# Attention and a two-layer MLP on one core: two blocks take w_in and x in float32, and w_in is split one block later

## The chip, the cores and the metric

The kernel runs on one core of one Trainium2 chip. A core has five engines with instruction queues of their own: TensorE (PE in the profile; its weight loads are PEld), VectorE (DVE), ScalarE (ACT), GpSimd (POOL) and SyncE (SP), which here only issues DMAs. The metric is the device time of one execution in microseconds (us); lower is better.

## The reference, cut to what matters

```python
q, k, v: (4, 8, 576, 64)          # batch, heads, sequence, head size; float32
q_rot, k_rot = rotate(q), rotate(k)
scores = np.matmul(q_rot, k_rot.transpose(0, 1, 3, 2)) / 8
attn = np.exp(scores - np.max(scores, axis=-1, keepdims=True))
attn = attn / (np.sum(attn, axis=-1, keepdims=True) + 1e-09)
attn_out = np.matmul(attn, v)
x = attn_out.transpose(0, 2, 1, 3).reshape(2304, 512)
h = x @ w_in                                             # w_in (512, 2048)
g = np.maximum(h, 0.0) + alpha * np.minimum(h, 0.0)
return g @ w_out                                         # w_out (2048, 512)
```

All in float32. The kernel is handed q and k with a turned copy beside them, and the bits of w_in and w_out as 64-bit floats.

## The kernel before, in words

**Tiles and blocks.** The 2304 tokens are 18 tiles of 128, and two tiles are a block: nine blocks. A block's attention is 16 heads: PE makes the scores (L655, or L683 where a tile holds the end of one batch and the start of the next), DVE their maximum (`mx`, L707), ACT the exponential (L716), ACT or DVE the float16 high part `pp` (L721, L354), DVE its low part (L735), a DMA transposes both (L739), and PE multiplies with v (L746). `normalise` divides (`y`, L761), splits y into two float16 parts `xs` (L765 or L766 high, L768 low), and a DMA transposes these to `xt` (L775).

**The two layers.** `expert(i, j)` does step j of 16 of block i. Layer 1 takes 128 columns of w_in: 12 float16 matmuls of 256 columns (L789: for each of four slices high by high, high by low, low by high) into the one buffer `h`; ACT and DVE make the leaky relu `r` (L800, L803), and not until both have read `h` can the next step's layer 1 begin. Layer 2 is in float32 for blocks 0 and 1 (L809, two matmuls of 512 columns, each of which the trace shows as two rows), and in three products of rounded parts from block 2 on (L827). `split(j)` makes w_out's parts in block 1's time (L609 high, L613 low; the low part is written into the buffer of step j-1, so it waits until block 1's layer 2 has used that).

**The weights.** `weights(g)`, for each quarter g: four pieces of w_in are loaded (L530), made into float32 by three integer operations on DVE (`to_f32`: L508, L513, L517), bounded (ACT takes absolute sums, L538; then a small chain on DVE and PE gives one scale `wsc` for the quarter), scaled and rounded to float16 on ACT (L582), and the low part is made on DVE (L586). The 64-bit buffer `wraw` (eight of them) is held until then. Four pieces of w_out are loaded, made into float32, and scaled by the bound on ACT (L599).

**What sets the order.** Every operation is handed to a planner (`Plan`) with a due time `at` (in steps; `slot(i, j)` is that of step j of block i, less an entry of the table `PRM`) and a cost for each engine that may do it. The planner plays the program through and writes one fixed order for each engine; engines with a choice get the operation that way. On the chip each engine runs its order as written and waits with semaphores.

Of the kernel before, what the change touches and what calls it, by code (L numbers as in the profile page):

```python
# [9 lines left out]
F32 = mybir.dt.float32  # L10
# [24 lines left out]
PRM = {"qd": 7.03, "qd0": 3.48, "vl0": 32.45, "wl": 12.02, "wl2": 12.07, "wb": 10.45, "wb2": 4.87, "ws": -0.7, "ws2": -0.08, "kl": 40.87, "vl": 40.84, "lead": 3.61, "flow": 4, "pen": -3.74, "ph": 1.2, "xlo": 1.8, "kd": 2.73, "pl": 1.01, "wlo": 16.77, "wg": 3.2, "bk": 1500, "lead1": 2.25, "ph0": 3.06, "nb": 1, "wh": 8.51, "lw": 3.8, "pvd": 4.03, "pw": 3.28, "la": 2, "lv": 1, "nks": 5, "nvv": 5, "ka": 2.03, "va": 0.1, "vc": -2.76, "vp": 1.47, "qa": 0.5, "qr": 78.54, "tqk": 1340, "l2d": 3.34, "tl2": 1400, "nos": 2, "nr": 2, "fo": 4, "fi": 4, "gh": 21.96, "gl": 10.88, "gh0": -1.64, "gl0": 1.86, "tp": 0, "nf": 2, "sh": 8.29, "sl": 2.28, "tl": 0, "wpe": 0, "vpe": 1, "wk": 4.09}  # L35
# [192 lines left out]
def t_dve(n, ap=0, fast=False):  # L228
    return 68 + (0.521 if fast else 1.042) * n + 60 * ap
# [6 lines left out]
def t_dma(size):  # L236
    return size / 360.0
# [3 lines left out]
def attention_moe(ctx: ExitStack, tc: tile.TileContext, q, k, v, w_in, w_out, alpha, tab, eye, out):  # L241
# [89 lines left out]
    e16_b = single("e16", [128, 128], F32)  # L331
# [5 lines left out]
    xu_T = tag("xu", 3, [128, 1], F32)  # L337

# [10 lines left out]
    def small(at, fn, reads=(), writes=()):  # L349
        op(at, {DVE: 75}, lambda e: fn(), reads=reads, writes=writes, port=False)  # L350
# [11 lines left out]
    def bound(at, cm, dst, acc, ps):  # L362
# [158 lines left out]

    def weights(g):
        at = slot(0, FG * g)
        wm, m, ps = wm_T.new(), column(at - 8), pair_T[1 + g % 2].new()
        raws = []
        for c in range(KC):
            raw, token = wr_T.new(), flow.new()
            raws.append((raw, token))
            op(at - PRM.get('wl', 16) + PRM.get('wg', 2) * g, {SP: t_dma(128 * 512 * 8)},
               lambda e, raw=raw, c=c: nc.sync.dma_start(  # L530
                   out=raw().rearrange("p f w -> p (f w)").bitcast(I64), in_=w_in[c, g]),
               writes=[raw, token])
        for c, (raw, token) in enumerate(raws):
            tmp = lambda c=c: wi_b().bitcast(I32)[:, c, g]
            dst = lambda raw=raw: raw()[:, :, 1]
            to_f32(at - PRM.get('wb', 5), raw, tmp, (wi_b, (c, g)), dst, raw, token)
            op(at - PRM.get('wb', 5), {ACT: t_act(512, ap=1)},
               lambda e, raw=raw, c=c, tmp=tmp: nc.scalar.activation(  # L538
                   out=tmp().bitcast(F32), in_=raw().bitcast(F32)[:, :, 1], func=ACTF.Abs,
                   accum_out=wm()[:, c:c + 1]),  # L540
               reads=[raw], writes=[(wi_b, (c, g)), (wm, c)])
        op(at - 4, {DVE: 80}, lambda e: nc.vector.tensor_reduce(out=m()[:, 0:1], in_=wm(), axis=AX.X, op=ALU.max),
           reads=[(wm, c) for c in range(KC)], writes=[m], port=False)
        bound(at - 4, m, lambda: we_b()[:, g:g + 1], (we_b, g), ps)
        we, wsc, wus = (lambda b=b: b()[:, g:g + 1] for b in (we_b, wsc_b, wus_b))
        scale_of(at - 4, wsc, (wsc_b, g), we, (we_b, g))
        small(at - 4, lambda: scalar(wus(), we(), 2.0**-14, None, ALU.mult), reads=[(we_b, g)], writes=[(wus_b, g)])
        by_pe = g < PRM["wpe"]
        if by_pe:
            dg = diagonal(at - 4, wsc, (wsc_b, g))  # L550
        for c, (raw, _) in enumerate(raws):
            f = lambda raw=raw: raw().bitcast(F32)[:, :, 1]
            t = lambda c=c: wi_b()[:, c, g]
# [428 lines left out]
```

## Time and profile before

| | |
|---|---|
| median of 3 runs (lowest to highest) | 688.65 us (685.98 to 691.06) |
| the profiled execution, its own time | 684.13 us |
| its span, first to last instruction | 682.3 us |
| mean granted TensorE clock | 0.955 of 2.4 GHz |
| busy in the span | PE 89%, DVE 74%, ACT 50%, POOL 27% |

The profile is one execution. A row of its timeline gives start, length, engine, line, operation and, in brackets, the time that the engine stood idle before it and what ended that. Lengths are from the start of one instruction to its end; one instruction may start a little before the end of the one ahead of it on its engine.

### The profile page before, as it was taken

The numbers are of one execution on the slowest core, as the hardware profiler recorded it, in microseconds if no ns is written. First come the engines' busy times: TensorE is split into PE (matmuls) and PEld (weight loads), VectorE is DVE, ScalarE is ACT, GpSimd is POOL, SyncE is SP. The second block draws the span as 40 slices with busy tenths as digits, with TensorE's granted clock in tenths as the row PEclk, the third lists the DMA queues.
The fourth block names the chain that finished last, engine by engine and source line by source line (L and its number), as shares of the span: only waits on it lengthen the run. The fifth ranks groups of instructions, "written<-read, shape, count | busy, mean of one in ns | idle before, by whom it ended". The sixth has DMA issues, their size and how long they took to land.

```text
span 682.3 us, 13828 instructions
## 1 busy us (share of the span) xinstructions
PE 608.4 (89%) x5384; PEld 443.8 (65%) x5384; DVE 507.9 (74%) x879; ACT 339.9 (50%) x766; POOL 181.0 (27%) x145
## 2 busy tenths in 40 slices
PE   0656678779899999999999999999999999999997
PEld 0334444455656567777767777677777777777775
DVE  5998999999778776768886586777866667765332
ACT  3536747539743435545654545464545445543322
POOL 4763000204642212126623222253211202110000
PEclk9966669979999999999999999999999999999999
DMA  8999898695985745468896456774445555462000
GB/s 302 312 233 226 159 292 214 193 272 121 222 167 108 135 86 132 86 114 184 198 211 106 99 118 103 112 183 100 84 69 105 110 78 86 101 119 54 32 0 32
DMA packets 209009, 96.47 MB, mean 141 GB/s; under 512 B 191792, under 2 KB 196016, under 8 KB 208944
## 3 DMA queue, kind: packets, MB, share of 16 engines
q1 hardware_dynamic: 208944, 95.59, 63.0%
q8 instruction: 42, 0.69, 0.4%
q14 instruction: 23, 0.19, 0.1%
HBM read 41.56 MB, written 4.72 MB: 68 GB/s over the span
## 4 chain that ended last, share of the span: by engine, by line
PE 68%; DMA 18%; DVE 10%; issue 1%; ACT 1%; SPq 1%; POOL 0%; ACTq 0%; DVEq 0%; POOLq 0%
PE h L789 24%; PE pair L827 21%; DMA pt<-pp 14%; PE v L746 8%; PE pair L655 8%; PE pair L809 5%; PE pair L683 2%; DVE kraw L390 1%; DMA qr<-in_q_dram 1%; DMA kraw<-in_k_dram 1%; DVE pp L735 1%; DVE mx L707 1%; DVE wi L586 1%; DMA wraw<-in_moe_w_out_dram 1%; DVE wraw L517 1%
## 5 line engine op out<-in xcount | busy, mean ns | idle before, releaser
L789 PE MATMUL h<-xt,wi 128*128 128x256 f16 x1728 | 231.4, 277 | 11.1 <-DVE r L803 10.6
L789 PEld LDWEIGHTS <-wi 128*128 128x128 f16 x1728 | 156.3, 99 | 72.3 <-issue 53.5
L716 ACT ACTIVATE e<-pair,mx 128x576 f32<-128x576 f32 x144 | 105.6, 736 | 87.7 <-DVE mx L707 83.5
L735 DVE SCALAR_TENSOR_TENSOR pp<-e,pp 128x576 f16<-128x576 f32 x144 | 126.1, 882 | 8.1 <-ACT pp L721 7.0
L803 DVE SCALAR_TENSOR_TENSOR r<-r,beta,h 128x256 f32<-128x256 f32 x144 | 68.7, 477 | 75.9 <-ACT r L800 75.6
L800 ACT ACTIVATE r<-h 128x256 f32<-128x256 f32 x144 | 55.1, 383 | 132.4 <-PE h L789 129.5
L746 PE MATMUL v<-vv,pt 128*128 128x64 f16 (+1 forms) x2240 | 92.6, 199 | 30.1 <-DMA pt<-pp 29.8
L746 PEld LDWEIGHTS <-pt 128*128 128x128 f16 (+1 forms) x2240 | 84.0, 104 | 51.3 <-DMA pt<-pp 41.6
L707 DVE TENSOR_REDUCE mx<-pair 128x1 f32<-128x576 f32 x144 | 103.2, 750 | 11.7 <-PE pair L655 10.3
L827 PE MATMUL pair<-wh,gh 128*128 128x512 f32 x224 | 96.0, 429 | 0.7 <-ACT gh L817 0.7
L655 PE MATMUL pair<-ks,qn 64*128 64x288 f32 x512 | 89.4, 453 | 7.2 <-ACT e L716 6.2
L827 PE MATMUL pair<-wh,gl 128*128 128x512 f32 x224 | 87.6, 391 | 0.8 <-POOL gl L820 0.8
L827 PE MATMUL pair<-wo,gh 128*128 128x512 f32 x224 | 88.2, 394 | 0.0
L820 POOL TENSOR_TENSOR gl<-r,gh 128x256 fp32r<-128x256 f32 x49 | 48.3, 986 | 116.5 <-ACT gh L817 80.1
L655 PEld LDWEIGHTS pair<-ks,qn 64*128 64x128 f32 x512 | 48.8, 196 | 35.5 <-issue 12.5
L721 ACT ACTIVATE pp<-e 128x576 f16<-128x576 f32 x90 | 61.1, 681 | 15.8 <-DMA pt<-pp 14.8
L817 ACT ACTIVATE gh<-r 128x256 fp32r<-128x256 f32 x97 | 40.4, 416 | 51.0 <-PE pair L827 33.9
L809 PE MATMUL pair<-wo,r 128*128 128x512 f32 x128 | 61.7, 607 | 0.0
L768 POOL TENSOR_TENSOR xs<-y,xs 128x512 f16<-128x512 f32 (+1 forms) x19 | 27.8, 1463 | 109.9 <-DVE xs L766 85.9
L827 PEld LDWEIGHTS pair<-wh,gl 128*128 128x128 f32 x224 | 42.0, 188 | 11.2 <-POOL gl L820 1.6
L827 PEld LDWEIGHTS pair<-wh,gh 128*128 128x128 f32 x224 | 42.2, 189 | 10.1 <-issue 1.9
L820 DVE TENSOR_TENSOR gl<-r,gh 128x256 fp32r<-128x256 f32 x63 | 28.7, 456 | 26.2 <-ACT gh L817 25.5
(77 smaller groups left out, 555.3 us busy)
## 6 DMA issues: line engine op xcount, KB each, us to landing
kraw<-in_k_dram SPq DMA_DIRECT2D x16, 576.0 KB, 4.6
qr<-in_q_dram SPq DMA_DIRECT2D x18, 512.0 KB, 4.2
wraw<-in_moe_w_in_dram SPq DMA_DIRECT2D x16, 512.0 KB, 5.5
wraw<-in_moe_w_out_dram SPq DMA_DIRECT2D x16, 512.0 KB, 5.6
vraw<-in_v_dram SPq DMA_DIRECT2D x16, 320.0 KB, 4.4
out_dram<-os SPq DMA_DIRECT2D x18, 256.0 KB, 2.2
pt<-pp SPq DMA_TRANSPOSE x144, 3.4
vv<-vv SPq DMA_DIRECT2D x32, 64.0 KB, 2.2
```

The lines of the kernel that those rows point to most:

```text
L655: nc.tensor.matmul(out=ps[h]()[:, x, :HS], lhsT=qn()[r, p], rhs=kt()[r, x * HS:(x + 1) * HS], start=True, stop=True)
L707: lambda e: nc.vector.tensor_reduce(out=mx()[a:z], in_=ps()[a:z, :, :HS], axis=AX.XY, op=ALU.max, negate=True),
L716: lambda e: nc.scalar.activation(out=ex()[a:z].rearrange("p (x c) -> p x c", x=2), in_=ps()[a:z, :, :HS], func=ACTF.Exp, bias=mx()[a:z], a ...
L721: lambda e: nc.scalar.activation(out=pp()[a:z, 0], in_=ex()[a:z], func=ACTF.Copy, scale=1.0 if early else E_SC) if e == ACT
L735: lambda e: nc.vector.scalar_tensor_tensor(out=pp()[a:z, 1], in0=ex()[a:z], scalar=E_SC, in1=pp()[a:z, 0], op0=ALU.mult, op1=ALU.subtract),
L746: nc.tensor.matmul(out=v_b()[c:d, 2 * p + g], lhsT=pt()[:, s, o:o + d - c], rhs=vt()[:, g, w], start=(n == 0), stop=(n == len(order) - 1))
L789: nc.tensor.matmul(out=ps(), lhsT=wi_b()[:, kk, j // FG, w, f], rhs=x()[:, y * KC + kk], start=(kk == 0 and n == 0), stop=(kk == KC - 1 an ...
L800: lambda e: nc.scalar.activation(out=g(), in_=ps(), func=ACTF.Relu, scale=-1.0),
L803: lambda e: nc.vector.scalar_tensor_tensor(out=g(), in0=g(), scalar=beta_b()[:, j:j + 1], in1=ps(), op0=ALU.mult, op1=ALU.add),
L809: nc.tensor.matmul(out=po()[:, x], lhsT=g()[:, x * 128:(x + 1) * 128], rhs=wf[j](), start=(j == 0), stop=(j == KF - 1))
L820: lambda e: ENG[e].tensor_tensor(out=gl(), in0=g(), in1=gh().bitcast(F32), op=ALU.subtract),
L827: nc.tensor.matmul(out=po()[:, x], lhsT=s()[:, ts], rhs=w, start=(j == 0 and c == 0), stop=(j == KF - 1 and c == 2))
```

## The change

Blocks 0 and 1 do layer 1 in float32 (`l1_f32`: 4 matmuls of 256 columns, from `w32`, w_in in float32 where its two float16 parts will lie later). Their x isn't split: `normalise` multiplies y's four 128-column pieces with the unit matrix on PE (`turn`), into the buffer of v, and ACT or DVE copies them to `xt`. `weights` stops after `to_f32` and the absolute sums, so `wraw` is free after these; w_out isn't scaled. One bound for all of w_in (`bound_w_in`) and the split of its 16 pieces (`split_in`: scaling to a buffer `os` of which there are two, high part, low part) come in block 1's time; the scale that w_out had goes into `xw` for the results of blocks 2 to 8. The planner's costs and table are others too (among them the cost of a DVE operation, 68 ns and now 130 ns ahead of the elements, and the look-ahead of queries and keys `la`, 2 and now 1).

```diff
-PRM = {..., "wb": 10.45, "wb2": 4.87, ..., "l2d": 3.34, ..., "la": 2, ...}
+PRM = {"si": 2.52, "sd": 6.06, ..., "wb": 9.81, "wb2": 3.64, ..., "l2d": 2.62, ..., "la": 1, ...}
...
     def weights(g):
...
-        bound(at - 4, m, lambda: we_b()[:, g:g + 1], (we_b, g), ps)
...
-            op(at - PRM.get('ws', 3), {ACT: t_act(512, ap=1)},
-               lambda e, f=f, t=t: nc.scalar.activation(
-                   out=t()[:, 0], in_=f(), func=ACTF.Copy, scale=wsc_b()[:, g:g + 1]),
-               reads=[raw, (wsc_b, g)], writes=[acc])
-            op(at - PRM.get('ws', 3), {DVE: t_dve(512, 1)},
-               lambda e, f=f, t=t: nc.vector.scalar_tensor_tensor(
-                   out=t()[:, 1], in0=f(), scalar=wsc_b()[:, g:g + 1], in1=t()[:, 0], op0=ALU.mult, op1=ALU.subtract),
-               reads=[raw, (wsc_b, g)], writes=[acc])
...
-               lambda e, w=w: nc.scalar.activation(out=w(), in_=w(), func=ACTF.Copy, scale=wus_b()[:, g:g + 1]),
...
+    def split_in(g):
+        at = slot(NF, FG * g) - PRM["si"]
+        for c in range(KC):
+            tmp, acc, t = os_T.new(), (wi_b, (c, g)), lambda c=c: wi_b()[:, c, g]
+            op(at, {ACT: t_act(512, ap=1), DVE: (t_dve(512, fast=True), PRM["sd"])},
+               lambda e, c=c, tmp=tmp: nc.scalar.activation(out=tmp(), in_=w32(c, g), func=ACTF.Copy, scale=wsc_b())
...
+            op(at, {ACT: t_act(512), DVE: (t_dve(512, fast=True), PRM["sd"])},
...
+            op(at, {POOL: t_pool(512, True), DVE: (t_dve(512), PRM["wlo"])},
+               lambda e, t=t, tmp=tmp: ENG[e].tensor_tensor(out=t()[:, 1], in0=tmp(), in1=t()[:, 0], op=ALU.subtract),
+               reads=[tmp], writes=[acc])
...
+            def turn(e):
+                for c in range(KC):
+                    w = slice(128 * c, 128 * c + 128)
+                    nc.tensor.matmul(out=vf()[:, w], lhsT=yf()[:, w], rhs=eye_b(), start=True, stop=True)
...
+        def l1_f32(e, half):
+            f = slice(j % FG * 128, (j % FG + 1) * 128)
+            for kk in range(half * KC // 2, (half + 1) * KC // 2):
+                nc.tensor.matmul(out=ps(), lhsT=w32(kk, j // FG)[:, f], rhs=x()[:, kk], start=(kk == 0), stop=(kk == KC - 1))
...
-    attention(NB, [(slot(0, FG * g) - PRM["wk"], g) for g in range(NG)])
+    for g in range(NG):
+        weights(g)
+    attention(NB)
...
             if i == NF - 1:
                 split(j)
+                if j == 0:
+                    bound_w_in()
+                if j % FG == FG - 1 and j < KF - 1:
+                    split_in(j // FG)
         result(i, po)
+        if i == NF - 1:
+            split_in(NG - 1)
```

In what follows the orders of three engines stand at three places. In a row `x2` means the same twice; `pair_778` is one PSUM buffer for scores. First DVE, from the division of tile 1's y to the first `r` of block 0, before:

```order
L761 TENSOR_TENSOR y<-v,rs 128x512
L517 SCALAR_TENSOR_TENSOR wo<-wraw,wo 128x512
L735 SCALAR_TENSOR_TENSOR pp<-e,pp 128x576
L586 SCALAR_TENSOR_TENSOR wi<-wraw,wsc,wi 128x512 x2
L735 SCALAR_TENSOR_TENSOR pp<-e,pp 128x576
L707 TENSOR_REDUCE mx<-pair_865 128x1
L586 SCALAR_TENSOR_TENSOR wi<-wraw,wsc,wi 128x512 x2
L707 TENSOR_REDUCE mx<-pair_867 128x1
```

And DVE's last rows ahead of that first `r` (L797) with the change:

```order
L518 SCALAR_TENSOR_TENSOR wo<-wraw,wo 128x512
L682 TENSOR_REDUCE mx<-pair_836 128x1
L509 TENSOR_SCALAR wi<-wraw 128x512
L682 TENSOR_REDUCE mx<-pair_838 128x1
L514 SCALAR_TENSOR_TENSOR wi<-wraw,wi 128x512
L797 SCALAR_TENSOR_TENSOR r<-r,beta,h 128x256
```

The low parts of w_in's first quarter (L586, four of them) are gone from between the heads' rows; what stands there is the making of float32. Next ACT in the middle of block 1's steps, before (L800 is `r`, L716 and L721 are the heads'):

```order
L716 ACTIVATE e,sums<-pair_2241,mx 128x576
L721 ACTIVATE pp<-e 128x576
L800 ACTIVATE r<-h 128x256
L716 ACTIVATE e,sums<-pair_2243,mx 128x576
L721 ACTIVATE pp<-e 128x576
L800 ACTIVATE r<-h 128x256 x2
```

And with the change (L794 is `r`, L691 a head's exponential, L566 the scaling to `os`, L570 the high part):

```order
L570 ACTIVATE wi<-os 128x512 x2
L794 ACTIVATE r<-h 128x256
L566 ACTIVATE os<-wi,wsc 128x512
L570 ACTIVATE wi<-os 128x512
L566 ACTIVATE os<-wi,wsc 128x512
L691 ACTIVATE e,sums<-pair_2195,mx 128x576
L570 ACTIVATE wi<-os 128x512
L794 ACTIVATE r<-h 128x256
```

Scalings and high parts of w_in now stand between one `r` and the next. Last POOL in the same stretch, before (L613 is w_out's low part):

```order
L613 TENSOR_TENSOR wo<-wo,wh 128x512 x2
L675 MEMSET qd 64x4x64
L632 TENSOR_TENSOR qr<-qr,tab 128x1024
L613 TENSOR_TENSOR wo<-wo,wh 128x512
L675 MEMSET qd 64x4x64
```

And with the change (L588 is w_out's low part, L574 that of w_in):

```order
L588 TENSOR_TENSOR wo<-wo,wh 128x512
L574 TENSOR_TENSOR wi<-os,wi 128x512 x4
L650 MEMSET qd 64x4x64 x2
L588 TENSOR_TENSOR wo<-wo,wh 128x512 x3
L574 TENSOR_TENSOR wi<-os,wi 128x512 x3
```

The low parts of w_in stand behind and between those of w_out; each of them sets one of the two `os` buffers free.

## Rows read from the trace of the kernel before

**Rows 1.** The page: busy us by engine, and the granted clock in 40 slices.

```profile
PE 608.4 (89%) x5384; PEld 443.8 (65%) x5384; DVE 507.9 (74%) x879; ACT 339.9 (50%) x766; POOL 181.0 (27%) x145
...
PEclk9966669979999999999999999999999999999999
```

**Rows 2.** Busy us by stretch: A, B, C, D (length, then engines, clock, DMA).

```profile
0.00:90.30 90.30, 46.75 (x358) 30.08 (x359) 76.61 (x113) 47.68 (x95) 38.66 (x29) 0.75 0.93 250
90.30:190.60 100.30, 83.26 (x634) 51.76 (x634) 95.10 (x183) 65.80 (x139) 25.96 (x19) 0.92 0.83 211
190.60:260.90 70.30, 68.44 (x622) 44.13 (x622) 54.37 (x88) 27.65 (x63) 18.97 (x15) 1.00 0.57 115
260.90:682.30 421.40, 409.99 (x3771) 317.81 (x3769) 281.78 (x500) 198.74 (x470) 97.44 (x83) 1.00 0.54 106
```

**Rows 3.** What PE waited for in 90.3 to 190.6: us, times, longest.

```profile
PE h L789 <- DVE r L803: 9.1, 5, 2.9
PE v L746 <- DMA pt<-pp: 6.6, 8, 2.1
```

**Rows 4.** DVE groups in 0 to 190.6: count, busy us, mean ns.

```profile
L735 DVE SCALAR_TENSOR_TENSOR pp<-e,pp 128x576 f16<-128x576 f32 x36 | 34.6, 967 | 2.4 <-ACT pp L721 2.4
...
L586 DVE SCALAR_TENSOR_TENSOR wi<-wraw,wsc,wi 128x512 f16<-128x512 f32 x16 | 13.4, 860 | 0.0
...
L393 DVE TENSOR_TENSOR ks<-kraw 128x576 f32<-128x576 f32 x5 | 6.5, 1303 | 0.1
...
L390 DVE TENSOR_TENSOR kraw<-kraw,tab 128x1152 f32<-128x1152 f32 x1 | 3.7, 3746 | 0.0
L354 DVE TENSOR_SCALAR e<-eye 128x128 f32<-128x128 f32 x1 | 1.4, 1422 | 0.0
L632 DVE TENSOR_TENSOR qr<-qr,tab 128x512 f32<-128x512 f32 x1 | 1.2, 1247 | 0.0
L366 DVE STREAM_TRANSPOSE ct<-cm 128x32 f32<-128x32 f32 x6 | 1.2, 207 | 0.0
...
L354 DVE TENSOR_SCALAR wus<-we 128x1 f32<-128x1 f32 x4 | 0.6, 142 | 0.0
```

**Rows 5.** DVE's timeline at the end of A.

```profile
78.67 0.68 DVE L761 TENSOR_TENSOR y<-v,rs 128x512 f32<-128x512 f32 x1
...
84.10 1.40 DVE L586 SCALAR_TENSOR_TENSOR wi<-wraw,wsc,wi 128x512 f16<-128x512 f32 x2
...
90.27 0.47 DVE L803 SCALAR_TENSOR_TENSOR r<-r,beta,h 128x256 f32<-128x256 f32 x1
```

**Rows 6.** DVE's timeline where C begins and ends.

```profile
190.58 0.47 DVE L803 SCALAR_TENSOR_TENSOR r<-r,beta,h 128x256 f32<-128x256 f32 x1
...
260.85 0.48 DVE L803 SCALAR_TENSOR_TENSOR r<-r,beta,h 128x256 f32<-128x256 f32 x1
```

**Rows 7.** POOL's timeline at tile 1's x, and the landing of its transposition.

```profile
80.17 1.47 POOL L768 TENSOR_TENSOR xs<-y,xs 128x512 f16<-128x512 f32 x1 [13.52 <-ACT xs L765]
...
xt<-xs SPq DMA_TRANSPOSE x1, 3.1
```

**Rows 8.** PE's timeline: block 0's first layer 1, and B.

```profile
85.17 2.72 PE L789 MATMUL h<-xt,wi 128*128 128x256 f16 x12 [0.23 <-DMA xt<-xs]
...
171.85 1.88 PE L809 MATMUL pair<-wo,r 128*128 128x512 f32 x4
...
175.89 1.47 PE L789 MATMUL h<-xt,wi 128*128 128x256 f16 x12
```

**Rows 9.** PE's float32 weight loads in 90.3 to 190.6.

```profile
L809 PEld LDWEIGHTS pair<-wo,r 128*128 128x128 f32 x64 | 11.6, 201 | 10.0 <-issue 8.8 <-DVE r L803 0.8
```

**Rows 10.** ACT's high parts of w_in in 0 to 190.6.

```profile
L582 ACT ACTIVATE wi<-wraw,wsc 128x512 f16<-128x512 f32 x16 | 11.4, 752 | 0.0
```

**Rows 11.** POOL and DVE groups in 190.6 to 260.9.

```profile
L613 POOL TENSOR_TENSOR wo<-wo,wh 128x512 fp32r<-128x512 f32 x9 | 13.0, 1447 | 43.7 <-PE pair L809 43.7
...
L735 DVE SCALAR_TENSOR_TENSOR pp<-e,pp 128x576 f16<-128x576 f32 x18 | 15.4, 862 | 1.7 <-ACT pp L721 1.6
```

More of the change, by code (lines that the diff above doesn't have):

```diff
@@ L236, in t_dma @@
 def t_dma(size):
-    return size / 360.0
+    return size / 340.0
 @with_exitstack
@@ L349, in small @@
     def small(at, fn, reads=(), writes=()):
[L350 removed]
+        op(at, {DVE: 150}, lambda e: fn(), reads=reads, writes=writes, port=False)
     def scalar(out, in0, s1, s2, op0, op1=None):
@@ L360, in column, with bound @@
         return cm
-    def bound(at, cm, dst, acc, ps):
+    def bound(at, cm, dst, acc, ps, place=lambda b: b[:, 0, HS:HS + 1]):
         ct, cr = ct_T.new(), cr_T.new()
@@ L532, in weights @@
                writes=[raw, token])
[L533 to L541, printed above, removed]
@@ L589, in weights @@
+            ti = lambda c=c: w32(c, g).bitcast(I32)
+            to_f32(at - PRM["wb"], raw, ti, acc, ti, acc, token)
+            op(at - PRM["ws"], {ACT: t_act(512, ap=1)},
+               lambda e, raw=raw, c=c: nc.scalar.activation(
+                   out=raw().bitcast(F32)[:, :, 1], in_=w32(c, g), func=ACTF.Abs, accum_out=wmax_b()[:, c, g:g + 1]),
+               reads=[acc], writes=[raw, (wmax_b, (c, g))])
         for j in range(g * FG, (g + 1) * FG):
@@ L763, in normalise @@
            reads=[rs] + [(vo, (h, a)) for h in range(H)], writes=[(y, a)], port=False)
+        if t < 2 * NF:
+            i, o = divmod(t, 2)
+            if i not in xt:
+                xt[i] = xt_T.new()
+                xt[i].make = lambda: xt_T.pool.tile([128, KC, 256], F32, name="xt", tag=f"xt{xt_T.opened % xt_T.bufs}")
+            yf, vf = lambda: y().rearrange("p h d -> p (h d)"), lambda: vo().rearrange("p h d -> p (h d)")
+            def turn(e):
+                for c in range(KC):
+                    w = slice(128 * c, 128 * c + 128)
+                    nc.tensor.matmul(out=vf()[:, w], lhsT=yf()[:, w], rhs=eye_b(), start=True, stop=True)
+            op(at, {PE: 1100}, turn, kind=WIDE, reads=[(y, a), eye_b], writes=[(vo, (h, a)) for h in range(H)])
+            op(at, {ACT: t_act(DM, True), DVE: (t_dve(DM), 2)},
+               lambda e: (nc.scalar.copy if e == ACT else nc.vector.tensor_copy)(
+                   out=xt[i]()[:, :, o * 128:(o + 1) * 128], in_=vf().rearrange("p (c n) -> p c n", c=KC)),
+               reads=[(vo, (h, a)) for h in range(H)], writes=[(xt[i], o)], port=False)
+            return
+        x2 = xss[t] = xss.get(t) or xs_T.new()
         op(at, {DVE: t_dve(DM, fast=True), ACT: t_act(DM)},
@@ L837, in result @@
             for b, s, a, z in tiles[t]:
+                u = xu[b]
+                if i >= NF:
+                    if b not in xw:
+                        xw[b] = xw_T.new()
+                        small(at - 4, lambda b=b: nc.vector.tensor_tensor(out=xw[b](), in0=xu[b](), in1=wus_b(), op=ALU.mult),
+                              reads=[xu[b], wus_b], writes=[xw[b]])
+                    u = xw[b]
                 op(at, {ACT: t_act(DM, True, 1)},
-                   lambda e, b=b, x=x, a=a, z=z, os=os: nc.scalar.activation(
-                       out=os()[a:z], in_=po()[a:z, x], func=ACTF.Copy, scale=xu[b]()[a:z]),
-                   reads=[(po, x), xu[b]], writes=[(os, a)])
+                   lambda e, u=u, x=x, a=a, z=z, os=os: nc.scalar.activation(
+                       out=os()[a:z], in_=po()[a:z, x], func=ACTF.Copy, scale=u()[a:z]),
+                   reads=[(po, x), u], writes=[(os, a)])
             op(at, {SP: t_dma(128 * DM * 4)},
@@ L907, in attention_moe @@
         result(i, po[i])
+    if NF == NB:
+        raise ValueError("the second block comes with float32 weights")
     for i in range(NB, len(blocks)):
```

107 lines of the change are left out of this document (35 added, 72 removed).

## The prediction

> **What bounds the kernel now.** I read the page first. PE is busy for 89% of the span and DVE for 74%, but the clock granted to PE falls to six tenths in several of the first ten slices and not once after them [rows 1]. So the kernel has at least two regimes, and I cut the span where block 0's, block 1's and block 2's first `r` starts: A up to 90.3, B to 190.6, C to 260.9, D to the end [rows 5, 6]. The table of these stretches [rows 2] shows who is full in each. In A, DVE is busy for 76.6 of 90.3 us, PE for 46.7. In B, DVE has 95.1 of 100.3 us, PE 83.3 at a mean clock of 0.92, and the DMA engines are busy for 0.83 of it: DVE is the bound, with PE close behind. In C, PE has 68.4 of 70.3 us and DVE 54.4; in D, PE has 410.0 of 421.4 and DVE 281.8. From 190.6 us on PE is the bound, and what is taken from DVE there is worth next to nothing. PE's waits in B confirm the reading: 9.1 us of layer 1 waiting for the DVE that makes `r`, and 6.6 us of the product with v waiting for transpositions whose input DVE makes [rows 3].
>
> So the change takes work from DVE, the bound of A and B, and adds work to PE, the bound of C and the runner-up in B.
>
> **The change part by part.**
>
> *A, DVE.* Removed up to the first `r`: four low parts of w_in at 0.86 us [rows 4], 3.4 us; one quarter's bound, eight small operations between 0.14 and 0.21 us [rows 4], 1.3 us; the scaled unit matrix, 1.4 us [rows 4]. By the order, DVE also does four operations less on raw keys and queries (1.25 to 1.30 us by the two rows shown, 5.1 us; POOL has them now) and one short one more, and two L735 (1.9 us) come after the first `r` instead of before. Against that, about one more piece of w_in is made float32 ahead of it, some 2.5 us (three operations, of a size with L586). The net is 9.4 to 10 us on DVE, if all of it was on the path. *A, the path of x.* Tile 1's y is done at 79.3 us and layer 1 starts at 85.17, released by the transposition [rows 5, 8]; POOL's low part (1.47 us) and a landing of 3.1 us lie between [rows 7]. Now four float32 matmuls of 128 columns stand there, and a copy like the ACT copies of this width. No row shows such a matmul; each will be two rows with a float32 weight load of 0.2 us [rows 9], eight loads in all, 1.6 us, and from above twice that, since layer 1's first twelve matmuls took 2.72 us in A and 1.47 later [rows 8]: with about 0.7 us for the copy, 2 to 3 us shorter. The four L586 that ended at 85.5 us, at the same time as the transposition, are gone too, so that neither takes the other's place. A lies between -2 (only the path of x) and -10 us (all of DVE's work); I take **-7**, nearer to DVE since DVE was 85% busy.
>
> *B, DVE.* Removed: twelve low parts, 10.3 us; three bounds, 3.8 us less 0.5 of the later one's; four `pp` that ACT does now and one maximum, some 3 us; 2.5 us of float32 making that came earlier. Added: the two L735, 1.9 us, and one product on keys that has a single row, 3.7 us, with POOL at work beside it [rows 4]. Net -15; DVE then needs 80 us. *B, PE.* A step's layer 1 was twelve matmuls in 1.47 us: 0.109 us from start to start (the last one's 0.27 us taken off). A float32 matmul of 512 columns is two rows 0.43 us apart (four rows in 1.88 us) [rows 8], so one of 256 columns should be two rows of 0.215, and a step 8 x 0.215 = 1.72 against 12 x 0.109 = 1.31 us: **+0.41 us a step**, 6.6 us a block. The weight loads (0.2 us each [rows 9]) just hide behind 0.215; were they not hidden, a step would be longer by little more than their overlap. Two turns add 3 us, three bounds less take 1.3 us off, and by the order two float32 matmuls of layer 2 and two of the scores move behind block 1's first layer 1 (four rows of 0.43 and four of 0.24, which is 0.43 scaled to 288 columns: 2.7 us). PE then needs 83.3 + 6.6 + 3.0 - 1.3 - 2.7 = 88.9 us at the same clock, and some 82 if the 8% that the clock lacked in B come back. B's new length lies between 82 (PE at full clock, DVE hidden) and 98 (PE's 88.9 and half of its present idle time); the two engines now need much the same, so waits stay. I take 90, near PE's own row: **-10**.
>
> ACT's high parts of w_in (16 x 0.75 us [rows 10]) and the scalings of w_out leave A and B; I cost this at nothing, since ACT is busy for 113 of 190.6 us there [rows 2], and it was DVE that it waited for. The `wraw` buffers come free earlier, and four x transpositions are gone; DMA has then a little more room, and that is in the 90 already.
>
> *C.* PE: +6.6 us for block 1's float32 layer 1, and the 2.7 us moved here: **+9.3**, all on the path since PE idled for only 1.9 us. The split of w_in lands in C and the first steps of D: on ACT 15 scalings and 15 high parts (some 20 us at 0.75 or a little less [rows 10]), on POOL 13 low parts of 1.45 us, on DVE three. ACT had 27.7 of 70.3 us, POOL 19.0, DVE 54.4 [rows 2]: I cost them at nothing, hidden by PE; if the cover fails, see the third rival. The single bound waits once for the `h` buffer, a microsecond or two, inside the uncertainty.
>
> *D.* Nothing of the change is in its matmuls; by the order the low part of `r` moves from DVE to POOL in 25 steps, on engines that are not the bound. 0, give or take 3.
>
> **Sum**: -7 - 10 + 9.3 = -8 us (rounded), against the profiled execution's 684.13 us (1.8 us outside its span): 676. The median of the runs is 4.5 us above that execution, so I put the change on the median: 688.65 - 8 = **680.6**. With the ends of A and B: from -10 - 18 + 9.3, 670, to -2 - 2 + 9.3, 694.
>
> **The rivals.**
>
> *1. PE takes DVE's place in B and nothing is gained there.* PE needs 88.9 us, its layer 1 still waits on one `h` buffer for ACT and DVE, and waits of PE in B were 17 us in all [rows 2]. If half stay, B shrinks by 2 us, and the sum is -7 - 2 + 9.3: **689**, no change. For it: the two engines come out almost equal. Against it: more than half of PE's idle time there was DVE's `r` [rows 3].
>
> *2. The clock comes back and both waits vanish.* B at 0.92 and A at 0.75 lost time on PE at the low of its two levels, 1.2 GHz. With PE fuller in B the clock might stay at 2.4 GHz: then B is 82 us and A gets its full 10: -10 - 18 + 9.3 = -19, **670**. The Trainium skill (TensorE: Matmul & The Clock Gate, section "Why this matters for your kernels") says that gaps between bursts of matmuls bring the clock back to half rate, which here would favour the fuller PE; the rows agree only in that the clock never falls in C and D, where PE has no gaps.
>
> *3. The split closes a ring in C, and the kernel gets slower.* By the order, POOL does w_in's low parts behind w_out's, and w_out's wait for PE: 43.7 us of such waits in C before, harmless since almost nothing stood behind [rows 11]. Now ACT's next scaling waits for one of two `os` buffers, which POOL sets free; behind it on ACT's queue stands the next `r`, and PE's next layer 1 waits for that. If each of POOL's 13 low parts is passed on in full, 13 x 1.45 = 18.9 us, the result is -8 + 19 = +11: **699**. It decides at the point where POOL ends a low part later than ACT reaches the scaling after the next. Against it: the order has one or two pieces to a step, and a step of C takes 70.3/16 = 4.4 us, now 4.8. The rule that speaks for it: L735 took 0.967 us in A and B, where POOL was busy for 64.6 us, and 0.862 in C [rows 4, 11]. The Trainium skill (SBUF — State Buffer, section "Who interferes with whom") says that a VectorE operation with two SBUF inputs and a GpSimd operation that reads SBUF exclude each other for a whole instruction; these rows agree with it in direction. By that rule 13 low parts could hold DVE up for 19 us, 54.4 + 19 = 73 of C's 77 us, which the sum survives and the ring doesn't.
>
> **How the numbers follow.** Forecast 0.50 (own range 674 to 687), rival 1 0.20, rival 2 0.18, rival 3 0.12. The range leaves out rival 3 and half of rival 2's cases below: 669 to 692. One per cent, about what a measurement of this kernel can tell from no change, is 6.9 us: below 681.8 is faster. The forecast lies close to that line: I give 0.33 of its 0.50 to faster and 0.17 to the same. Rival 1 gives 0.18 to the same and 0.02 to slower, rival 2 0.17 to faster and 0.01 to the same, rival 3 0.10 to slower and 0.02 to the same. Faster 0.50, same 0.38, slower 0.12.
>
> **What would show it.** In the profile after: the first `r` near 83 us (A); block 1's first `r` near 173 (B), with DVE and PE both about 90% busy between; rows of float32 layer 1 about 0.215 us apart, eight to a step; C about 77 to 80 us long with PE idle for 2 or 3; D within 3 us of 421. Rival 1 shows as B near 98 with PE waiting for ACT or DVE; rival 2 as a clock of 1.00 in B; rival 3 as PE waiting in C for `r`, with ACT waiting for POOL at L566. The prediction is wrong above all if B doesn't shrink, or if a float32 step of layer 1 costs much more than 1.72 us.

## The result, and the profile after

The changed kernel takes **681.0 us** (median of 4 runs, 678.3 to 682.95) beside 689.4 for the kernel before on the same chip (4 runs, 685.98 to 691.06): a ratio of 0.9888, 95% interval 0.9857 to 0.9918. That is 1.1% faster, and the interval leaves no change out. The forecast was 680.6. The traced execution of the kernel before (684.1 us) was faster than all its timed ones and that of the changed kernel (682.95 us) the slowest of its own, so the first two traces differ by only 1.2 us where the medians differ by 8.4.

The page of the changed kernel: busy us by engine, and the granted clock. It answers to [rows 1].

```profile
PE 624.8 (92%) x5282; PEld 461.0 (68%) x5282; DVE 482.6 (71%) x803; ACT 341.6 (50%) x772; POOL 227.8 (33%) x187
...
PEclk9957589799999999999999999999999999999999
```

PE has 16 us more work, DVE 25 less, POOL 47 more. The stretches A to D, cut at the same three `r` (now L797), are the answer to [rows 2]; the columns are the same (length; PE, PEld, DVE, ACT, POOL busy; clock, DMA share, GB/s).

```profile
0.00:91.80 91.80, 50.82 (x366) 33.30 (x367) 64.30 (x98) 41.23 (x87) 42.79 (x29) 0.74 0.92 242
91.80:181.00 89.20, 83.96 (x572) 55.92 (x570) 80.33 (x140) 48.73 (x110) 20.41 (x14) 0.96 0.80 226
181.00:260.20 79.20, 79.15 (x580) 53.01 (x579) 61.95 (x100) 45.56 (x93) 40.12 (x30) 1.00 0.44 107
260.20:680.90 420.70, 410.87 (x3771) 318.76 (x3769) 276.06 (x469) 206.04 (x483) 124.43 (x115) 1.00 0.47 106
```

**A** didn't shrink, though DVE's work in it fell from 76.6 to 64.3 us. **B** is 11.1 us shorter and **C** 8.9 longer, both close to the forecast. In B both engines are nearly full (PE 94%, DVE 90%); in C PE idles for 0.05 us. What PE still waits for in B (us, times, longest), beside 9.1 and 6.6 us in [rows 3]:

```profile
PE h L777 <- DVE r L797: 4.0, 3, 1.6
PE pair L630 <- ACT e L691: 1.1, 1, 1.1
```

The price of float32 in layer 1, on PE's timeline (start, length, what); it answers to [rows 8]:

```profile
84.94 1.52 PE L744 MATMUL v<-eye,y 128*128 128x128 f32 x8
...
88.33 3.02 PE L777 MATMUL h<-xt,wi 128*128 128x256 f32 x8 [1.87 <-ACT xt L748]
...
204.20 1.89 PE L777 MATMUL h<-xt,wi 128*128 128x256 f32 x8
205.93 0.59 PE L803 MATMUL pair<-wo,r 128*128 128x512 f32 x1
```

A step is eight rows and takes PE 205.93 - 204.20 = 1.73 us; the prediction had 1.72. The turn takes 1.52 us at A's clock, a little under the 1.6 to 3.2 that was forecast.

Why A didn't shrink begins with what DVE waited for in it (us, times, longest), of the changed kernel:

```profile
DVE pp L705 <- ACT pp L696: 13.7, 6, 3.9
DVE neg L355 <- DMA eye<-in_eye_dram: 5.1, 1, 5.1
DVE beta L858 <- DMA alpha<-in_moe_alpha_dram: 3.6, 1, 3.6
```

In the kernel before, the first of these was

```profile
DVE pp L735 <- ACT pp L721: 2.3, 4, 0.9
```

And ACT's `pp` waits in turn, 13.8 us where it was 8.6 before, for a transposition to set a `pp` buffer free:

```profile
ACT pp L696 <- DMA pt<-pp: 13.8, 6, 4.1
```

So DVE's waiting grew by about what its work shrank, beside DMA engines that are busy for 0.92 of A as they were for 0.93 before. This alone doesn't show that the one turned into the other: the order of the operations changed too.

### The profile page after: what moved, and what is told of

Same layout as the page of the kernel before. It is cut to its first block, busy times and chain, and to the rows that moved or that the text cites. A ratio compares the mean times of both kernels' runs of the same rounds, so it can differ in the third digit from the quotient of the medians.

```text
span 680.9 us, 13592 instructions
## 1 busy us (share of the span) xinstructions
PE 624.8 (92%) x5282; PEld 461.0 (68%) x5282; DVE 482.6 (71%) x803; ACT 341.6 (50%) x772; POOL 227.8 (33%) x187
## 4 chain that ended last, share of the span: by engine, by line
PE 78%; DMA 10%; DVE 7%; SPq 2%; issue 2%; ACT 1%; POOL 0%; ACTq 0%; DVEq 0%; POOLq 0%
PE pair L821 21%; PE h L783 20%; PE v L716 9%; PE pair L630 9%; PE h L777 8%; PE pair L803 7%; DMA pt<-pp 6%; PE pair L658 2%; DVE pp L705 2%; DMA wraw<-in_moe_w_in_dram 1%; PE pair L468 1%; DVE mx L682 1%; DMA kraw<-in_k_dram 1%; SPq L709 1%; DMA qr<-in_q_dram 1%
## 5 line engine op out<-in xcount | busy, mean ns | idle before, releaser
L783 PE MATMUL h<-xt,wi 128*128 128x256 f16 x1344 | 174.6, 273 | 2.1 <-DVE r L797 2.0
L705 DVE SCALAR_TENSOR_TENSOR pp<-e,pp 128x576 f16<-128x576 f32 x144 | 133.6, 936 | 23.9 <-ACT pp L696 22.5
L783 PEld LDWEIGHTS <-wi 128*128 128x128 f16 x1344 | 119.5, 98 | 44.3 <-issue 31.7
L691 ACT ACTIVATE e<-pair,mx 128x576 f32<-128x576 f32 x144 | 105.9, 738 | 59.8 <-DVE mx L682 56.7
L797 DVE SCALAR_TENSOR_TENSOR r<-r,beta,h 128x256 f32<-128x256 f32 x144 | 68.7, 477 | 89.7 <-ACT r L794 88.5
L794 ACT ACTIVATE r<-h 128x256 f32<-128x256 f32 x144 | 55.1, 383 | 148.3 <-PE h L783 109.9
L814 POOL TENSOR_TENSOR gl<-r,gh 128x256 fp32r<-128x256 f32 x74 | 61.8, 835 | 161.4 <-ACT gh L811 148.5
L716 PEld LDWEIGHTS <-pt 128*128 128x128 f16 (+1 forms) x2240 | 83.8, 104 | 46.3 <-DMA pt<-pp 27.0
L682 DVE TENSOR_REDUCE mx<-pair 128x1 f32<-128x576 f32 x144 | 103.5, 750 | 15.0 <-PE pair L630 10.3
L716 PE MATMUL v<-vv,pt 128*128 128x64 f16 (+1 forms) x2240 | 91.8, 199 | 20.3 <-DMA pt<-pp 18.4
L630 PE MATMUL pair<-ks,qn 64*128 64x288 f32 x512 | 90.4, 460 | 6.7 <-ACT e L691 5.7
L821 PE MATMUL pair<-wh,gl 128*128 128x512 f32 x224 | 88.5, 395 | 0.0
L777 PE MATMUL h<-xt,wi 128*128 128x256 f32 x256 | 67.7, 403 | 5.9 <-DVE r L797 4.0
L811 ACT ACTIVATE gh<-r 128x256 fp32r<-128x256 f32 x104 | 43.3, 417 | 57.5 <-DVE r L797 37.6
L630 PEld LDWEIGHTS pair<-ks,qn 64*128 64x128 f32 x512 | 49.6, 200 | 31.7 <-issue 11.1
L696 ACT ACTIVATE pp<-e 128x576 f16<-128x576 f32 x90 | 61.1, 680 | 17.0 <-DMA pt<-pp 13.8
L777 PEld LDWEIGHTS h<-xt,wi 128*128 128x128 f32 x256 | 47.9, 196 | 19.6 <-DVE r L797 8.1
L821 PEld LDWEIGHTS pair<-wh,gl 128*128 128x128 f32 x224 | 42.0, 187 | 10.3
```

The costliest lines, as they stand in the source:

```text
L630: nc.tensor.matmul(out=ps[h]()[:, x, :HS], lhsT=qn()[r, p], rhs=kt()[r, x * HS:(x + 1) * HS], start=True, stop=True)
L682: lambda e: nc.vector.tensor_reduce(out=mx()[a:z], in_=ps()[a:z, :, :HS], axis=AX.XY, op=ALU.max, negate=True),
L691: lambda e: nc.scalar.activation(out=ex()[a:z].rearrange("p (x c) -> p x c", x=2), in_=ps()[a:z, :, :HS], func=ACTF.Exp, bias=mx()[a:z], a ...
L696: lambda e: nc.scalar.activation(out=pp()[a:z, 0], in_=ex()[a:z], func=ACTF.Copy, scale=1.0 if early else E_SC) if e == ACT
L705: lambda e: nc.vector.scalar_tensor_tensor(out=pp()[a:z, 1], in0=ex()[a:z], scalar=E_SC, in1=pp()[a:z, 0], op0=ALU.mult, op1=ALU.subtract),
L716: nc.tensor.matmul(out=v_b()[c:d, 2 * p + g], lhsT=pt()[:, s, o:o + d - c], rhs=vt()[:, g, w], start=(n == 0), stop=(n == len(order) - 1))
```

## The experiments

**Both kernels again.** What the lengths of A to D are worth was to be known first.

> The changed kernel as it is, for a second trace beside the first, whose four stretches A to D were 91.8, 89.2, 79.2 and 420.7 us against 90.3, 100.3, 70.3 and 421.4 before. Theory: B shorter by about 11 us and C longer by about 9 come back within 2 us, and A (where transpositions wait for DMA) stays within 4 us of 91.8, so that what the first trace lacks of the median gain of 8 us is this execution's scatter. Rival: A is shorter by 5 us or more in other executions, the 7 us that I forecast, and 91.8 was an outlier.

> The kernel before as it is, for a second trace. Theory: the profiled execution of before (684.1 us) was at the low end of its runs (686 to 691); a trace near the median has A or B longer by some 4 to 5 us, while C and D, bound by TensorE, stay within 1 us of 70.3 and 421.4. Rival: all four stretches are longer in proportion.

One run each: 677.6 us for the changed kernel, 689.1 for the one before. A and D of the first, then A and D of the second:

```profile
0.00:91.10 91.10, 48.63 (x372) 31.96 (x373) 66.79 (x99) 41.57 (x87) 43.13 (x29) 0.74 0.92 244
...
258.40:675.60 417.20, 410.25 (x3771) 318.04 (x3769) 275.04 (x469) 206.13 (x483) 123.41 (x115) 1.00 0.48 107
```

```profile
0.00:91.80 91.80, 50.41 (x358) 32.40 (x359) 77.27 (x113) 48.07 (x95) 38.24 (x29) 0.74 0.94 247
...
262.80:687.30 424.50, 409.66 (x3771) 317.69 (x3769) 282.15 (x500) 198.85 (x470) 96.36 (x83) 1.00 0.54 105
```

B was 88.1 and 100.8, C 79.2 and 70.2. The mean of two traces each, before and after: A 91.05 and 91.45, B 100.55 and 88.65, C 70.25 and 79.2, D 422.95 and 418.95. So A +0.4, B -11.9, C +9.0, D -4.0; the sum, -6.5, stands beside -8.4 between the medians. B and C differ by far more than two runs of one kernel do; D's difference is about the 3.5 and 3.1 us between two runs of one kernel (it had been expected to stay within 1 us). But most of the kernels further down leave D's work and order as they are, and their traces can be counted too: with the changed kernel's D it took 417.2 to 421.3 us in eight traces (mean 419.5), with that of the kernel before 421.4 to 424.5 in three (mean 423.1). So most of the 4 us stands.

**Table against structure.** The diff changes the work and also the table and costs from which the order is planned. One kernel has the old work with the new table and costs, one the new work with the old ones:

```diff
-PRM = {"qd": 7.03, ..., "la": 2, ...}
+PRM = {"si": 2.52, "sd": 6.06, ..., "la": 1, ...}
...
-    return 68 + (0.521 if fast else 1.042) * n + 60 * ap
+    return 130 + (0.521 if fast else 1.042) * n + 50 * ap
...
-    return size / 360.0
+    return size / 340.0
...
-        op(at + 0.3, {SP: 1010 if z - a == 128 else 505},
+        op(at + 0.3, {SP: 1100 if z - a == 128 else 550},
```

The second has the same lines the other way round, and keeps the new table's entries for the split of w_in.

> The kernel before with the changed kernel's table and costs in the planner, its work left as it was (all in float16 parts, w_in split in block 0's time). Theory that the moved work makes the gain: within 4 us of the kernel before, 685 to 694. Rival that the table and the costs make it: 679 to 684.

> The changed kernel's work in an order planned with the table and costs of before (only the two new entries of the table added). Theory that the moved work makes the gain: 679 to 685, B near 90 us. Rival that the table and costs make it: 688 or more, with B back near 100 us or C far above 80.

Both are slower than the kernel before: ratios 1.0148 (1.0103 to 1.0192) and 1.0093 (1.0060 to 1.0126). That the moved work makes the gain under any order is refuted. But the trades show in each: with the old work, B is 101.1 and C 73.7; with the new work under the old table, B is 86.0. The second loses elsewhere, its A and C:

```profile
0.00:95.70 95.70, 52.31 (x388) 34.25 (x389) 83.03 (x116) 43.12 (x90) 40.85 (x27) 0.77 0.95 258
...
181.70:272.10 90.40, 84.58 (x580) 56.11 (x579) 66.65 (x114) 40.95 (x86) 30.10 (x22) 0.96 0.46 105
```

In this C, POOL's low parts and PE wait (us, times, longest):

```profile
POOL wi L574 <- DVE wi L571: 12.6, 1, 12.6
...
POOL wi L574 <- PE h L777: 6.4, 1, 6.4
...
PE v L716 <- DMA vv<-vv: 3.8, 3, 2.1
```

PE idles there for 5.8 us and its clock is 0.96, where the changed kernel has 0.05 us and 1.00. A third kernel keeps the changed kernel's work and table, with the old costs alone:

```diff
-    return 130 + (0.521 if fast else 1.042) * n + 50 * ap
+    return 68 + (0.521 if fast else 1.042) * n + 60 * ap
```

> The changed kernel with its own table but with the planner's cost functions of before. If the table carries what the old one lost (693.7 us with both old), this is 679 to 685; if the costs carry it, 690 or more. A structure that gains by itself whatever the order would leave both within 4 us of 681, and the run with both old has already spoken against that.

Its ratio is 0.9983 (0.9950 to 1.0016): no change against the kernel before. Its 686.2 us lie between the 679 to 685 and the 690 or more that were expected, so the table and the costs each carry about 1%. B is 84.5 and C 81.7, but A is 98.6 us. In all three the work, the table and the costs don't belong together, and all three lose in A: 95.7 to 99.6 us, where both kernels have 90 to 92.

DVE's wait for `pp` in A goes with the order and not with the work. First the old work in the new order, then the new work in the old one:

```profile
DVE pp L735 <- ACT pp L721: 12.8, 6, 3.4
```

```profile
DVE pp L705 <- ACT pp L696: 0.3, 1, 0.3
```

So the 13.7 us of the changed kernel (10.0 in its second trace) are not simply the removed work come back as waiting: the old work waits as long in this order. In A the two halves of the change meet. A of the old work with the new table and costs:

```profile
0.00:99.60 99.60, 49.93 (x384) 31.87 (x385) 72.61 (x115) 49.83 (x100) 45.72 (x32) 0.72 0.90 242
```

The new table and costs lengthen the old work's A by some 8.5 us, and under them the new work shortens it by some 8; under the old ones the new work lengthens it by 4.7 (91.05 to 95.7). What the moved work is worth in A hangs on the order.

**Half of float32 layer 1.** Each step does two of its four float32 matmuls, so half of the contraction is left out in blocks 0 and 1.

```diff
-            for kk in range(half * KC // 2, (half + 1) * KC // 2):
+            for kk in [half * KC // 2]:
```

> The changed kernel in the same order, but layer 1 of blocks 0 and 1 leaves out every second of its four float32 matmuls (half of the contraction isn't computed there), 0.86 us less on TensorE in each of 32 steps. Theory: C is TensorE's alone, so its 79.2 us become 66 to 68, while B is held by VectorE as much as by TensorE and gives back 0 to 5 of its 13.8; 662 to 667 in all. Rival, that B too is TensorE's: B from 88.5 to 78 or less, 655 to 659 in all.

Ratio 0.9757 (0.9708 to 0.9805), 671.7 us, where 662 to 667 was expected. B and C:

```profile
90.50:176.40 85.90, 76.57 (x508) 45.96 (x508) 79.10 (x140) 49.65 (x112) 20.59 (x14) 0.91 0.86 235
176.40:247.40 71.00, 67.24 (x512) 40.19 (x513) 62.10 (x99) 43.29 (x91) 42.16 (x30) 1.00 0.54 118
```

16 steps x 4 rows x 0.215 = 13.8 us of PE's work are gone from each. C gives 8 of them back, not the 11 to 13 expected, and then waits for `r` and for transpositions (PE idles for 3.8 us): PE holds C as the forecast had it, down to a next bound at 71. B gives back only 2.7 of 13.8. The granted clock fell to 0.91 there, so that PE's busy time shrank by 7 us and not by 13.8; yet PE now idles for 9.3 us of B, so it is not PE's work that holds B.

**DVE's work doubled in one place.** The third operation of `to_f32` for w_in is done twice: 6 more operations in A, 10 in B, 0.6 us each from start to start.

```diff
+            for _ in range(2 if dst_acc is tmp_acc and isinstance(dst_acc, tuple) else 1):
                 nc.vector.scalar_tensor_tensor(
                     out=dst(), in0=raw()[:, :, 1], scalar=-0x40000000, in1=tmp(),
```

> The changed kernel in the same order, with the last integer operation on each piece of w_in done twice on VectorE (0.60 us each, as much as the low part that the change took away; the result is the same): 6 of them in A, 10 in B. Theory: VectorE idles in A for 27 us waiting behind transpositions, so A stays within 2 us; B is held by VectorE and grows by 5 to 6 us: 685 to 687 in all. Rival, that B is now TensorE's: B grows by under 2 us, 679 to 683.

Ratio 0.9995 (0.9967 to 1.0022): the gain is gone. A and B:

```profile
0.00:92.10 92.10, 49.79 (x368) 32.30 (x368) 66.74 (x104) 41.62 (x87) 43.00 (x29) 0.76 0.89 241
92.10:184.90 92.80, 82.72 (x566) 55.30 (x567) 87.66 (x149) 48.76 (x110) 20.39 (x14) 0.96 0.75 217
```

In B 6.0 us of DVE's work cost 4.2; in A 3.6 us cost 0.6. By the lengths of their rows the additions are larger, 4.2 us in A and 10.2 in B, where single ones last up to 2.9 us. DVE still holds B, and in this trace has slack in A. But the whole runs lost some 7 us against the changed kernel (by the two ratios) and the stretches of this trace only 4.4: the traced run took 684.7 us beside a median of 687.3, so both costs may be too low.

**What holds A.** First the transpositions of `pp` of block 0 alone, at 640 of 1152 columns; PE then multiplies some columns twice and leaves others out.

```diff
-           lambda e: nc.sync.dma_start_transpose(out=pt()[:, :, :z - a], in_=pp()[a:z]...),
+               out=pt()[:, :5 if t < 2 else NSEG, :z - a],
+               in_=pp()[a:z].rearrange("p x c -> p (x c)")[:, :640 if t < 2 else 2 * S]),
```

> The changed kernel in the same order, but the DMA transpositions of block 0's 16 heads move 640 of their 1152 columns, and the products with v read those in place of the rest (so block 0's attention isn't the reference's). Theory: in A the heads wait for transpositions and these share the DMA engines with the loads, so A is shorter by 6 us or more and the wait of ScalarE's high parts for transpositions (13.8 us) falls by half or more. Rival, that A is held by the order on VectorE and GpSimd: A within 2 us of 91.5.

A and B:

```profile
0.00:88.40 88.40, 50.61 (x368) 32.68 (x368) 69.81 (x98) 41.81 (x87) 44.41 (x29) 0.79 0.80 228
88.40:174.40 86.00, 80.38 (x565) 53.74 (x566) 79.88 (x140) 48.28 (x110) 20.38 (x14) 1.00 0.82 234
```

The transpositions land after 3.4 us in place of 5.0, DVE's waits for `pp` fall from 13.7 to 5.7 us, and A falls to 88.4: three us, half of what was expected. B, in which nothing was changed, took 86.0 us at a granted clock of 1.00. Next, every load of a weight piece is cut to 256 of 512 columns, so that half of the weights' values are others; alone, and with the short transpositions.

```diff
-                   out=raw().rearrange("p f w -> p (f w)").bitcast(I64), in_=w_in[c, g]),
+                   out=raw()[:, :256].rearrange("p f w -> p (f w)").bitcast(I64), in_=w_in[c, g][:, :256]),
```

> The changed kernel with every load of a w_in or w_out piece cut to its first 256 of 512 columns (256 KB in place of 512 KB); the making of float32 then reads these columns twice, at the same size, and the order of every engine is that of the changed kernel. Half of the weights' values are therefore other ones. 14 of these pieces are loaded in A of the changed kernel (22.2 MB moved there), so 3.6 MB, 16% of the bytes, go. Theory (in A the DMA engines' load is a bound, and the transpositions of pp land late because they share them): the landing of pt<-pp falls from 5.0 to about 4 us, A falls from 91.5 by 5 us or more, B by 1 to 3. Rival (A is a chain through DVE, ACT and PE that the transpositions only end): the landing may fall, A changes by less than 2 us and DVE's or PE's other waits grow.

> The same cut of the loads, and block 0's transpositions of pp at 640 of 1152 columns as in the run before with short transpositions (A 88.4 there, against 91.5). Theory (the DMA engines bound A): the two cuts add up, A falls to 80 or below, DVE's idle time on pp nearly vanishes, and A then ends by DVE's busy time of 65 to 70 us and its waits. Rival (a chain through DVE, ACT and PE): A stays at 87 or above though the DMA engines' busy share falls well below 0.8.

A was 87.8 (transpositions landing after 4.1 us) and 85.8. Each number fell between the two theories: what the DMA engines carry is a bound of A, worth 6 us, but not all of it. So the same two cuts were made in the kernel before, and DVE's doubled operations were tried with both cuts.

> The kernel before with the same two cuts (each load of a w_in or w_out piece 256 of 512 columns, block 0's transpositions of pp 640 of 1152), its orders unchanged; the third operation of to_f32 reads its own intermediate in place of the raw word, at the same size. With both cuts the changed kernel's A was 85.8. Theory (the change took DVE's work out of A, and the DMA engines' landings took its place): the kernel before gains little from the cuts, since DVE still holds it with 76.6 us of work, and its A is 89 to 91, so that with the DMA engines eased the change is worth 3 to 5 us in A. Rival (DVE's work held A in neither kernel): its A falls as much as the changed kernel's did, to 85 or 86.

> The changed kernel with both cuts, and the third operation of to_f32 for w_in done twice, as in the earlier run with 16 such operations: six of them lie in A (0.6 us each, 3.6 us) and ten in B (6 us). Without the cuts the six cost A 0.6 us. Theory (with the DMA engines eased DVE is the next bound of A): A goes from 85.8 to 88 or more. Rival (A is then a chain in which DVE has slack): A stays below 87. B should grow by about 4 us either way, from 90.1 to 94.

A with both cuts, for the changed kernel, the kernel before, and the changed kernel with six more DVE operations:

```profile
0.00:85.80 85.80, 50.70 (x368) 32.91 (x368) 68.94 (x99) 41.67 (x87) 44.69 (x29) 0.80 0.75 201
```

```profile
0.00:88.50 88.50, 46.36 (x358) 29.33 (x359) 78.39 (x112) 47.77 (x95) 40.68 (x29) 0.79 0.77 202
```

```profile
0.00:91.00 91.00, 52.34 (x366) 33.97 (x367) 73.23 (x104) 41.69 (x87) 42.78 (x29) 0.79 0.69 190
```

With DMA eased the kernel before gains 2.5 us in A and the changed kernel 5.7, so that A is 2.7 us shorter with the change, and no shorter without the cuts. The theory's 89 to 91 and its 3 to 5 us are missed by a little, the rival's 85 or 86 by 2.5. The third row is the clearer: the six operations, which cost 0.6 us before the cuts, cost 5.2 after them. Their own rows are longer here (twelve of this operation take 10.3 us, where six took 4.0), and the traced run is the slowest of its five, 2.3 us above their median, so part of the 5.2 is scatter. Work added to DVE does lengthen A as soon as the transpositions land earlier. B grew from 90.1 to 92.7, where 94 was expected.

Where the 2.7 us lie is told by the starts of three operations (us): the division of tile 1's y, block 0's first layer 1, and the first `r`, which ends A.

| trace | y | layer 1 | `r` |
|---|---|---|---|
| before, two traces | 78.7, 80.0 | 85.2, 86.5 | 90.3, 91.8 |
| old work, new table and costs | 81.8 | 90.1 | 99.6 |
| changed, two traces | 82.8, 81.7 | 88.3, 87.1 | 91.8, 91.1 |
| before, both cuts | 77.7 | 84.2 | 88.5 |
| changed, both cuts | 77.6 | 82.3 | 85.8 |
| changed, both cuts, DVE's additions | 81.3 | 86.8 | 91.0 |

With both cuts the two kernels reach y at the same time: of the 2.7 us, 1.8 are the path from y to layer 1 and 0.9 the way from there to `r`. Up to y the 9.5 us less work on DVE bought nothing even then, though the additions cost 3.7 us there. Without the cuts the changed kernel gains on the same two ways, 1.0 and 1.5 us, and reaches y 3 us later; the cuts bring its y forward by 4.6 us, and that of the kernel before by 1.7. Against the old work with the new table, too, all that the new work gains lies behind y.

What DVE waits for in A of the changed kernel with both cuts:

```profile
DVE neg L355 <- DMA eye<-in_eye_dram: 4.7, 1, 4.7
DVE pp L707 <- ACT pp L698: 4.0, 3, 2.7
DVE beta L862 <- DMA alpha<-in_moe_alpha_dram: 3.6, 1, 3.6
```

The whole kernels with cuts took 678.5 (loads), 677.9 (transpositions), 677.7 (both), 683.0 (the kernel before with both) and 683.7 us (with DVE's additions). In the first and third of these B grew by 1.3 and 1.5 us over the changed kernel's mean, so that part of what A gained was lost again one stage later; in the second it shrank by 2.7. The whole runs don't confirm that the change is worth more with the cuts: beside the kernel before on the same chip the changed kernel with both is 9.9 us shorter and the kernel before with both 7.2, so 2.7 apart (with intervals of some 3 us on each), where it is 8.4 without. The 2.7 us in A rest on one trace of each kernel.

## Why the prediction was right, and which of its steps was not

**A: the failed step is the -7, "nearer to DVE since DVE was 85% busy".** The size of the removed work was right: 9.4 to 10 us by the forecast, 12.3 and 10.5 in the two pairs of traces, 78.39 - 68.94 = 9.5 between the two kernels with both cuts. What was wrong is what it would buy: A stayed (+0.4). The forecast took DVE for the one bound of A, though the same row of [rows 2] had the DMA engines at 0.93. It asked what is late next for PE, the path of x, but not what sets DVE's own inputs free: `pp` waits for a buffer until the transposition of an earlier one has landed (4.5 us in the kernel before, 5.0 after), and in the new order DVE waits for `pp` for 13.7 us. Cutting both kinds of transfer shortens A by 5.7 us, and only then does work added to DVE lengthen it by about as much; so the transfers are shown to hold A in part. The transfers account for a part of the -7 only: with the cuts A is 2.7 us shorter with the change, and none of that lies ahead of tile 1's y. The order is the other part: with the new table and costs the old work's A is 99.6 us, and against that the new work gains some 8 us, all behind y. So a gain of the forecast's size is there under the new table and costs, which took as much away by themselves; the forecast counted the operations that the order moves, but not what the order does to the waits. How the missing 7 us divide between the order and the transfers, and what holds the rest, stays open. DVE's first waits in the changed kernel with both cuts, for `eye` and `alpha` (8.3 us together, where the kernel before with both cuts waits 6.2 for keys), are two of its parts.

The path of x, the lower end of the range for A, became 1.0 us shorter, where 2 to 3 were worked out: from y's start at 82.83 us to layer 1 at 88.33 are 5.5 us, and 78.67 to 85.17 were 6.5 in [rows 5, 8]. The turn had its price, but it and the copy came late. DVE's, PE's and ACT's timelines there, of the changed kernel:

```profile
82.83 0.69 DVE L731 TENSOR_TENSOR y<-v,rs 128x512 f32<-128x512 f32 x1
```

```profile
82.72 2.29 PE L630 MATMUL pair<-ks,qn 64*128 64x288 f32 x8
```

```profile
87.06 0.67 ACT L537 ACTIVATE wraw<-wi 128x512 f32<-128x512 f32 x1 [4.12 <-DVE wi L518]
...
87.71 0.57 ACT L748 COPY xt<-v 128x512 f32<-128x512 f32 x1
```

The turn (84.94) stands behind eight rows of scores on PE's queue, 1.4 us after y was done. The copy stands behind an absolute sum of w_in, which waits 4.12 us for DVE; PE waits 1.87 us for that copy.

**B: right.** -10 was forecast and -11.9 measured. DVE needs 80.3 us (forecast 80; its terms in the forecast add up to -13.5 and not -15, which would be 81.6), PE 84.0 at a clock of 0.96 (forecast 88.9 at 0.92 and 82 at full clock). PE's two largest waits went from 15.7 us [rows 3] to 5.1. Of the two nearly equal engines DVE holds B more than PE: the doubled operations cost 4.2 of 6.0 us there, half of layer 1's float32 work gave 2.7 of 13.8 back. PE's clock counts as well: at 1.00, in the one trace with the short transpositions, B took 86.0 us with the same work on DVE.

**C: right.** +9.3 was forecast and +9.0 measured, all of it on PE: 10.7 us more work in 9.0 us more time, its 1.9 us of idle time used up. The forecast had 1.4 us less work and left PE 2 or 3 us idle; these two misses cancel, which is luck. The split of w_in was hidden, as costed: PE waited for nothing.

**D: 0 was forecast, -4.0 came out** on the mean of two traces each that differ by 3.5 and 3.1 us, and -3.6 with all traces that have one D or the other. PE's busy time in it is within 1.3 us in the first four, so it is PE's idle time that shrank. The old work with the new table has 419.1 and the new work with the old table 420.3, one trace each, so the runs don't tell whether the work or the order gives it; the cause stays open. It made up for about half of what A lacked, and B's 2 us for some more. **The sum was right with one term that was wrong by 7 and two that were wrong by 2 and 4 the other way: that the forecast came within 1 us is luck.**

**Rival 1** (PE takes DVE's place in B, which then gains nothing) is refuted: B shrank, and the two experiments on B leave DVE as the fuller bound. **Rival 2** (the clock comes back) came true by a half: in B, where PE's busy share rose from 83 to 94%, the clock went from 0.92 to 0.96; in A, where PE is busy for 55% and waits in between as before, it stayed at 0.74. B at full clock is worth less than the rival had it: at 1.00 it was the 86.0 us above, not 82. That the clock rose where PE's gaps shrank agrees with what the prediction cited from the Trainium skill (TensorE: Matmul & The Clock Gate, "Why this matters for your kernels"). **Rival 3** (the ring in C) was not met. Who waits in C of the changed kernel:

```profile
POOL wo L588 <- PE pair L803: 31.0, 10, 9.9
...
ACT os L566 <- POOL wi L574: 1.1, 2, 0.8
```

POOL waits for PE, as before [rows 11], but ACT waits for an `os` buffer for 1.1 us in all. With the old table it was another matter (C 90.4): there the low parts of w_in did get stuck, behind DVE and PE rather than behind w_out's alone, so that something like the rival's ring lies one order away. Its rule on DVE and POOL bears on C too. The groups in C of the changed kernel (count, busy us, mean ns):

```profile
L705 DVE SCALAR_TENSOR_TENSOR pp<-e,pp 128x576 f16<-128x576 f32 x18 | 19.1, 1068 | 2.5 <-ACT pp L696 2.4
```

This operation took 862 ns before, with POOL busy for 19.0 us of C; now POOL is busy for 40.1 us and it takes 1068. The Trainium skill (SBUF — State Buffer, "Who interferes with whom") says that a VectorE instruction with two SBUF inputs contends with a GpSimd instruction that reads SBUF, and the rows agree in direction: 18 x 0.206 = 3.7 us more for DVE, and PE covers them.

The forecast was put on the median and not on the first trace, and that was needed: the first two traces differ by only 1.2 us.

## What to carry to other kernels

Before work is taken from the busiest engine of a stretch, look at every column that is as high, DMA's share too, and ask what sets that engine's inputs and buffers free: here some 10 us less work on DVE bought nothing in A, beside DMA engines that were as full and in an order that had changed with it. The test for it is cheap: add a known piece of work to the engine there, and see how much of it the stretch grows by (B by 4.2 of 6.0 us, A by 0.6 of 3.6). A test that adds work doesn't say what removing work buys: with the transfers cut, additions cost A nearly their full length, and the removal still brought nothing up to tile 1's y. A change that comes with a new table for the order is to be judged with that table: the same work under the other order was 2% slower here.

## What the runs showed of the hardware

The transposition of one `pp` (128 x 1152, float16) landed after 5.0 us in A of the changed kernel, after 4.1 with the weights' loads beside it halved, after 3.4 with 640 columns, and after 3.1 with both: halving the loads beside it took 0.9 us off, and 44% of its own columns 1.6. The granted clock of PE in A rose with each of these cuts (from 0.74 to 0.79, 0.79 and 0.80), with the same matmuls in it.
